# Blocks 0 and 1 of a retention-plus-FFN kernel in units of 256 tokens and four heads, with two tokens per partition

## The chip, the cores and the metric

The kernel runs on one core of a Trainium2 chip. The metric is the device time of one execution in microseconds (us); of several runs the median is taken.

## The reference

Two layers follow each other. The first is a recurrent attention with decay (retention): for 4 batches, 8 heads, 768 tokens and a head dimension of 64, a 64 x 64 state per head is decayed by gamma and takes up the outer product of k and v at each token; y is q times the state. The second is a feed-forward pair over the 3072 tokens, with x of 512 columns (8 heads x 64), 2048 hidden columns, and a PReLU whose slope for negative values is alpha.

```python
for t in range(S):
    state = gamma[None, :, None, None] * state + np.einsum('bhd,bhe->bhde', k[:, :, t], v[:, :, t])
    y[:, :, t] = scale * np.einsum('bhd,bhde->bhe', q[:, :, t], state)
...
h = x @ w_in
g = np.maximum(h, 0.0) + alpha * np.minimum(h, 0.0)
return (g @ w_out).astype(np.float32)
```

Inputs and output are float32; the kernel computes its matmuls in float16 with float32 sums.

## The kernel before, in words

The recurrence is cut into chunks of 128 tokens. Within a chunk it is a masked product of scores; between chunks a state per pair of heads is carried. A unit u is one chunk of one batch with all 8 heads, 24 units in all; four units make a block of 512 tokens, and the feed-forward pair runs once per block (`ffn1`, `ffn2`; six blocks).

For each unit:

- `load` (L109) issues three DMAs of 256 KB on SP's queue: k, q, v, one token per partition, so that each packet is one token of one head, 256 bytes. Eight buffers per tensor.
- `prep` scales k (L127, on VectorE for the first two blocks, later on GpSimd) and q (L135, GpSimd) by the decay tables into `kdq`, and casts v into `vx` (L149, GpSimd). `vx` has a block of zeros in the middle, so that a 128-column slice of it holds one head of a pair and zeros for the other.
- `stage_a` turns k and q (eight 128 x 128 transposes on TensorE, L168, for the first 10 units, a transposing DMA for the others), ScalarE copies the result to `kq` (L175), and k times v gives the chunk's state in PSUM (`stp`, L181). VectorE adds it to the carried state (L193, L197, two calls of 64 rows, the diagonal 64 x 64 squares alone), GpSimd multiplies by the decay of 128 tokens (L199) into `tg`, the state for the next chunk.
- `stage_b` computes the scores (L214, eight matmuls that each use 64 of TensorE's rows) and masks them on VectorE (L224).
- `stage_c` computes y transposed (L239, L246 within the chunk, L254 from the carried state) into `yps`; ScalarE copies it to `xT` (L264).

`ffn1` runs 16 hidden tiles with four 512-column matmuls each (L282); ScalarE (L292) and VectorE (L293) form the PReLU into `gt`. `ffn2` (L321) sums 16 tiles for four groups of 128 tokens, ScalarE evacuates (L330) and issues the store (L334). With parts=4 it goes through the 16 tiles in four rounds, so that a round needs one quarter of w_out.

Each engine takes its instructions in the order in which the program issues them, written out by hand here: `tick(gen, m)` issues the next m matmuls of a generator, with the stages of attention between such pieces. `keep(m)` issues m spin matmuls (L95) on data that nothing uses. In block 0 the units run before any feed-forward work, each with keep(5). The weights come over GpSimd's queue: w_in in five DMAs (L361), w_out in four quarters (L365). Their issues stand between GpSimd's own products. The loads of units 4 to 11 wait on SP until the first quarter of w_out has landed (`held`). While ffn2 of block n runs, the units of block n+1 are computed. PSUM has two groups of four banks, "pa" (attention) and "pb" (ffn); a tile takes the next bank of its group when its last user is done.

Of the kernel before, what the change touches and what calls it, by code (L numbers as in the profile page):

```python
# [9 lines left out]
FP = mybir.dt.float32  # L10
# [8 lines left out]
def kernel(  # L19
# [27 lines left out]
    NTAB = 2 * H + NP + 16  # L47
# [4 lines left out]
    for p in range(NP):  # L52
        tab_np[0:64, 2 * H + p] = g64[2 * p] ** 128
        tab_np[64:128, 2 * H + p] = g64[2 * p + 1] ** 128
    tab_np[0:NFT, NTAB - 16 : NTAB] = np.eye(NFT)
    tab_np = tab_np.astype(np.float32)
    mi_np = np.zeros((128, 256), dtype=np.float16)
    mi_np[:, 0:128] = p_ar[:, None] <= p_ar[None, :]
    mi_np[:, 128:256] = np.eye(128)

# [8 lines left out]
    mi = sbp.tile([128, 256], F16, tag="mi", name="mi")  # L69
    mask = mi[:, 0:128]  # L70
    ident = mi[:, 128:256]
    alpha_sb = sbp.tile([NFT, 128], FP, tag="alpha", name="alpha")
# [8 lines left out]
    NPE = 10  # L81
    vext = [sbp.tile([128, NP, 3, 64], F16, tag=f"vx{i}", name=f"vx{i}") for i in range(NV)]
# [21 lines left out]
    def load(u):  # L104
        b, c = divmod(u, NCH)
        t = {}
        for nm, src in (("k", k), ("q", q), ("v", v)):
            t[nm] = sbp.tile([128, H, D], FP, tag=f"{nm}s", bufs=8, name=f"{nm}s{u}")
            ins = nc.sync.dma_start(  # L109
                out=t[nm],  # L110
                in_=src[b, :, C * c : C * c + C, :].rearrange("h p d -> p h d"),
            )
# [11 lines left out]
    def prep(u, ahead=None, amid=None, behind=None):  # L124
        t = staged.pop(u)
        kdq = sbp.tile([128, 2, H, D], F16, tag="kdq", bufs=8, name=f"kdq{u}")
        (nc.vector if u < 2 * UB else nc.gpsimd).tensor_tensor(  # L127
            out=kdq[:, 0],
            in0=t["k"],
            in1=tab[:, 0:H].unsqueeze(2).to_broadcast([128, H, D]),  # L130
            op=MULT,
        )
        if ahead:
            ahead()
        nc.gpsimd.tensor_tensor(  # L135
            out=kdq[:, 1],
            in0=t["q"],
            in1=tab[:, H : 2 * H].unsqueeze(2).to_broadcast([128, H, D]),
            op=MULT,
        )  # L140
        if amid:
            amid()
# [10 lines left out]
        if behind:  # L153
            behind()
# [6 lines left out]
    def stage_a(u):  # L161
# [16 lines left out]
        if c < NCH - 1:  # L178
# [11 lines left out]
            for lh in range(2):  # L190
                s = slice(64 * lh, 64 * lh + 64)
                if c > 0:
                    nc.vector.tensor_tensor(  # L193
                        out=new[s, :, s], in0=tgs[u][s, :, s], in1=stv[s, :, s], op=ADD
                    )
                else:
                    nc.vector.tensor_copy(out=new[s, :, s], in_=stv[s, :, s])  # L197
# [148 lines left out]
    for u in range(UB):  # L346
        load(u)
# [149 lines left out]
```

## Time and profile before

| what | us |
|---|---|
| three runs: median (lowest, highest) | 230.56 (229.25, 231.67) |
| the profiled execution, its own time | 228.91 |
| its span, first to last instruction | 227.1 |
| TensorE busy | 211.8 |
| VectorE busy | 124.8 |
| ScalarE busy | 96.1 |
| GpSimd busy | 83.1 |
| first transposes of units 0, 1, 2, 3 (L168) | 6.20, 9.82, 13.28, 17.12 |
| first matmul of ffn1, of ffn2 in block 0 (L282, L321) | 21.51, 36.25 |
| first transpose of block 2, right behind ffn1 of block 1 | 77.69 |
| last evacuation (L330) starts | 223.07 |

In the profile, PE is TensorE, PEld its weight loads, DVE VectorE, ACT ScalarE, POOL GpSimd, SP the queue of the loads. A row of the groups names line, engine, operation, tiles and shapes, then total busy time and the mean duration of one in ns, then the idle time ahead of it and what ended it. The slices cut the span into 40 equal parts and give the busy share in tenths. The chain follows the work that ended last back to its start. The DMA view gives packets, megabytes, and the time of the packets as a share of 16 engines over the window; several packets of one engine can be in flight, so the shares can add up to more than 100%.

### The profile page before, as it was taken

To read this page: it belongs to the slowest core of one execution; us is meant where nothing else is said; L and a number is where in the kernel's file an instruction comes from. 1 tells how busy PE (TensorE), PEld (TensorE's weight loads), DVE (VectorE), ACT (ScalarE), POOL (GpSimd) and SP (SyncE) were. 2 spreads that over 40 slices of the span, in tenths; PEclk is the share of its full clock that TensorE was granted. 3 is DMA by queue.
4 is the path that set the end of the run, shared out by engine and by line. 5 is a ranking of instruction groups with operands and counts; after the bars stand their busy time and mean duration, and the time that the engine had idled before them with its cause. 6 is when DMAs were issued, how large, how long until landed. Compare 5 with 4: busy or idle time off the path is not lost.

```text
span 227.1 us, 3793 instructions
## 1 busy us (share of the span) xinstructions
PE 211.8 (93%) x1454; PEld 108.5 (48%) x1454; DVE 124.8 (55%) x203; ACT 96.1 (42%) x156; POOL 83.1 (37%) x99
## 2 busy tenths in 40 slices
PE   7786998949889999999999999999999999999992
PEld 2454644525454555544455544455544555544440
DVE  4485496431539845248855268834288834288100
ACT  2242673411737732256522367323376231566121
POOL 2689302632496134950031990104970230000000
PEclk9999999999999999999999999999999999999999
DMA  7999999998999999699911399931470011100111
GB/s 156 218 200 160 199 189 225 207 186 182 283 275 218 193 211 253 154 263 226 198 48 49 93 245 224 229 92 46 104 161 15 0 62 58 67 3 0 46 66 73
DMA packets 98209, 33.36 MB, mean 147 GB/s; under 512 B 90368, under 2 KB 95120, under 8 KB 98192
## 3 DMA queue, kind: packets, MB, share of 16 engines
q1 hardware_dynamic: 89664, 22.55, 50.6%
q0 software_dynamic: 4752, 4.19, 12.1%
q10 hardware_dynamic: 3776, 6.39, 7.9%
q8 instruction: 11, 0.18, 0.3%
q14 instruction: 6, 0.05, 0.1%
HBM read 27.36 MB, written 6.29 MB: 148 GB/s over the span
## 4 chain that ended last, share of the span: by engine, by line
PE 73%; DMA 13%; POOL 5%; SPq 4%; ACT 2%; issue 1%; ACTq 0%; POOLq 0%
PE ops L321 33%; PE hps L282 31%; DMA wout<-in_moe_w_out_dram 8%; DMA qs<-in_q_dram 4%; SPq L109 4%; PE sca L214 3%; PE yps L246 2%; PE yps L239 2%; PE yps L254 1%; POOL win L361 1%; POOL kdq L135 1%; POOL tg L199 1%; PE stp L181 1%; ACT kq L175 1%; ACT os L330 1%
## 5 line engine op out<-in xcount | busy, mean ns | idle before, releaser
L321 PE MATMUL ops<-wout,gt 128*128 128x512 f16 x384 | 92.5, 379 | 3.1 <-DMA wout<-in_moe_w_out_dram 3.1
L293 DVE SCALAR_TENSOR_TENSOR gt<-hm,oma,hps 128x512 f16<-128x512 f32 x96 | 69.8, 746 | 31.2 <-ACT hm L292 23.3
L282 PE MATMUL hps<-xT,win 128*128 128x512 f16 (+2 forms) x416 | 84.6, 363 | 1.7 <-ACT xT L264 1.7
L292 ACT ACTIVATE hm<-hps 128x512 f32<-128x512 f32 x96 | 56.7, 597 | 23.4 <-PE hps L282 22.8
L282 PEld LDWEIGHTS <-win 128*128 128x128 f16 x416 | 39.3, 98 | 45.3 <-issue 2.5
L321 PEld LDWEIGHTS <-gt 128*128 128x128 f16 x384 | 34.5, 98 | 38.0 <-issue 3.7
L199 POOL TENSOR_TENSOR tg<-ss,tab 128x512 f16<-128x512 f32 x20 | 20.9, 1043 | 70.7 <-DVE ss L193 50.2
L135 POOL TENSOR_TENSOR kdq<-qs,tab 128x512 f16<-128x512 f32 x24 | 25.3, 1054 | 30.3 <-DMA qs<-in_q_dram 30.3
L330 ACT ACTIVATE os<-ops 128x512 f32<-128x512 f32 x24 | 14.3, 596 | 46.3 <-PE ops L321 42.8
L224 DVE TENSOR_TENSOR m<-sca,mi 128x512 f16<-128x512 f32 x24 | 16.6, 691 | 28.4 <-PE scb L214 28.1
L264 ACT ACTIVATE xT<-yps 128x512 f16<-128x512 f32 x24 | 14.3, 597 | 36.2 <-PE yps L254 32.1
L175 ACT ACTIVATE kq<-trb 128x1024 f16<-128x1024 f16 x10 | 10.2, 1024 | 19.4 <-PE trb L168 18.9
L193 DVE TENSOR_TENSOR ss<-tg,stp 64x256 f32<-64x256 f16 x32 | 13.4, 418 | 8.5 <-PE stp L181 5.6
L127 POOL TENSOR_TENSOR kdq<-ks,tab 128x512 f16<-128x512 f32 x16 | 16.7, 1044 | 0.4 <-DMA ks<-in_k_dram 0.4
L239 PE MATMUL yps<-m,vx 128*128 128x128 f16 x96 | 16.8, 219 | 0.0
L246 PE MATMUL yps<-m,vx 128*128 128x128 f16 x96 | 16.6, 219 | 0.0
L224 DVE TENSOR_TENSOR m<-scb,mi 128x512 f16<-128x512 f32 x24 | 16.3, 680 | 0.0
L149 POOL CAST vx<-vs 128x512 f16<-128x512 f32 x24 | 14.7, 612 | 2.0 <-DMA vs<-in_v_dram 1.7
L127 DVE TENSOR_TENSOR kdq<-ks,tab 128x512 f16<-128x512 f32 x8 | 6.4, 800 | 14.7 <-DMA ks<-in_k_dram 14.7
L254 PE MATMUL yps<-kq,tg 128*128 128x128 f16 x80 | 14.4, 219 | 0.0
L246 PEld LDWEIGHTS <-vx 128*128 128x128 f16 x96 | 9.4, 98 | 2.3
L239 PEld LDWEIGHTS <-vx 128*128 128x128 f16 x96 | 9.4, 98 | 2.3
(26 smaller groups left out, 85.2 us busy)
## 6 DMA issues: line engine op xcount, KB each, us to landing
ks<-in_k_dram SPq DMA_DIRECT2D x24, 256.0 KB, 4.4
qs<-in_q_dram SPq DMA_DIRECT2D x24, 256.0 KB, 4.7
vs<-in_v_dram SPq DMA_DIRECT2D x24, 256.0 KB, 5.1
out_dram<-os ACTq DMA_DIRECT2D x24, 256.0 KB, 2.0
wout<-in_moe_w_out_dram POOLq DMA_DIRECT2D x4, 512.0 KB, 10.3
win<-in_moe_w_in_dram POOLq DMA_DIRECT2D x3, 512.0 KB, 6.8
win<-in_moe_w_in_dram POOLq DMA_DIRECT2D x2, 256.0 KB, 4.6
kq<-kdq SPq DMA_TRANSPOSE x14, 4.1
```

The lines of the kernel that those rows point to most:

```text
L127: (nc.vector if u < 2 * UB else nc.gpsimd).tensor_tensor(out=kdq[:, 0], in0=t["k"], in1=tab[:, 0:H].unsqueeze(2).to_broadcast([128, H, D]) ...
L135: nc.gpsimd.tensor_tensor(out=kdq[:, 1], in0=t["q"], in1=tab[:, H : 2 * H].unsqueeze(2).to_broadcast([128, H, D]), op=MULT,)
L199: nc.gpsimd.tensor_tensor(out=tg, in0=new, in1=tab[:, 2 * H : 2 * H + NP].unsqueeze(2).to_broadcast([128, NP, 128]), op=MULT,)
L224: nc.vector.tensor_tensor(out=m2, in0=scs[lh].rearrange("p (a i) -> p a i", i=128), in1=mask.unsqueeze(1).to_broadcast([128, NP, 128]), op ...
L239: nc.tensor.matmul(out=o, lhsT=vx[:, p, 0:2, :].rearrange("p a d -> p (a d)"), rhs=m2s[0][:, p, :], start=True, stop=False,)
L246: nc.tensor.matmul(out=o, lhsT=vx[:, p, 1:3, :].rearrange("p a d -> p (a d)"), rhs=m2s[1][:, p, :], start=False, stop=(c == 0),)
L254: nc.tensor.matmul(out=o, lhsT=tgs[u][:, p, :], rhs=kq[:, 512 + 128 * p : 512 + 128 * p + 128], start=False, stop=True,)
L282: nc.tensor.matmul(out=hpss[ft][:, lo:hi], lhsT=w_in_all[:, hp, 128 * ft : 128 * ft + 128], rhs=xT[n][:, hp, lo:hi], start=(hp == 0), stop ...
L292: nc.scalar.activation(out=hm, in_=hps, func=RELU, bias=0.0, scale=-1.0)
L293: nc.vector.scalar_tensor_tensor(out=gt[:, ft, :], in0=hm, scalar=oma_sb[:, ft : ft + 1], in1=hps, op0=MULT, op1=ADD,)
L321: nc.tensor.matmul(out=opss[tq], lhsT=gt[:, ft, 128 * tq : 128 * tq + 128], rhs=w_out_all[:, ft, :], start=(ft == 0), stop=(ft == NFT - 1),)
L330: nc.scalar.activation(out=os_sb, in_=opss[tq], func=COPY, bias=0.0, scale=1.0)
```

## The change

Blocks 0 and 1 get units of another shape. Unit i = 2j + g is 256 tokens (chunks 2j and 2j+1) of four heads (group g), the same 256 KB per tensor. A partition holds two neighbouring tokens, so a packet is 512 bytes. The first 64 partitions are the first chunk (half 0), the others the second (half 1); s tells the even from the odd token. The attention of such a unit uses 64-row matmuls for the state (`u_state`) and for the part within the chunk (`u_out`), and 64 x 64 tiles for the scores (`u_scores`). `u_turn` does the transposes, in block 0 with ScalarE's copy in two pieces (parts=2). `uprep` scales k on VectorE and q on GpSimd; v is cast on ScalarE in block 0, on GpSimd in block 1.

Beside that: five units are loaded ahead of the weights instead of four; w_in comes in four DMAs of 512 KB, the first after q's product of unit 3, the other three after the state product of unit 3; in all units the state is added in one call over 128 x 512 (or 128 x 256) with the off-diagonal squares, which the product with the new table `gmat` sets to zero; the first part of `ffn1` in blocks 0 and 1 starts with one hidden tile over 256 tokens instead of four over 384; and block 1's pieces stand at other places in ffn2 of block 0. Blocks 2 to 5 keep their units and their order.

The diff, cut to its core ("..." marks what is left out):

```diff
         for nm, src in (("k", k), ("q", q), ("v", v)):
+            st = sbp.tile([128, H * D], FP, tag=f"{nm}s", bufs=8, name=f"{nm}s{u}")
+            if u < NUN:
+                j, g = divmod(u, 2)
+                b, c = divmod(2 * j, NCH)
+                t[nm] = st.rearrange("p (h s d) -> p s h d", s=2, d=D)
+                ins = nc.sync.dma_start(
+                    out=st.rearrange("p (h x) -> p h x", h=H // 2),
+                    in_=src[
+                        b, H // 2 * g : H // 2 * g + H // 2, C * c : C * c + 2 * C, :
+                    ].rearrange("h (p s) d -> p h (s d)", s=2),
+                )
...
                 )
             new = sst[u % NT]
             stv = stp.rearrange("p (a e) -> p a e", e=128)
-            for lh in range(2):
-                s = slice(64 * lh, 64 * lh + 64)
-                if c > 0:
...
+            if c > 0:
+                nc.vector.tensor_tensor(out=new, in0=tgs[u], in1=stv, op=ADD)
+            else:
+                nc.vector.tensor_copy(out=new, in_=stv)
+            tg = sbp.tile([128, NP, 128], F16, tag="tg", bufs=4, name=f"tg{u}")
+            nc.gpsimd.tensor_tensor(out=tg, in0=new, in1=gmat, op=MULT)
             tgs[u + 1] = tg
...
+    def uprep(i, amid=None, behind=None, cast=None):
...
+        for a, (eng, nm) in enumerate(((nc.vector, "k"), (nc.gpsimd, "q"))):
+            o = TU + 2 * H * a
+            eng.tensor_tensor(
+                out=kdu[:, a],
+                in0=t[nm],
+                in1=tab[:, o : o + 2 * H]
+                .rearrange("p (s h) -> p s h", s=2)[:, :, H // 2 * g : H // 2 * g + H // 2]
+                .unsqueeze(3)
+                .to_broadcast([128, 2, H // 2, D]),
+                op=MULT,
+            )
+        if amid:
+            amid()
+        vx = vext[i % NV].rearrange("p (s r) x d -> p s r x d", s=2)
+
...
+    def u_turn(i, tag="pa", parts=1):
+        kdu, kq, vx, cast_v = prepped[i]
+        trb = ps("trb", F16, 1024, tag=tag)
+        for x in range(2 * NP):
+            a, s, r = x // NP, x // 2 % 2, x % 2
+            nc.tensor.transpose(
+                out=trb[:, 128 * x : 128 * x + 128],
+                in_=kdu[:, a, s, 2 * r : 2 * r + 2, :].rearrange("p a d -> p (a d)"),
+                identity=ident,
+            )
+            if (x + 1) % (2 * NP // parts) == 0:
+                lo = 128 * (x + 1 - 2 * NP // parts)
+                hi = 128 * (x + 1)
+                nc.scalar.activation(
+                    out=kq.rearrange("p a i -> p (a i)")[:, lo:hi],
+                    in_=trb[:, lo:hi],
+                    func=COPY,
+                    bias=0.0,
+                    scale=1.0,
+                )
+
+    def u_state(i, tagb="pa"):
+        j, g = divmod(i, 2)
+        kdu, kq, vx, cast_v = prepped[i]
+        ua = 2 * j
+        b, ca = divmod(ua, NCH)
+        halves = (0, 1) if ca + 1 < NCH - 1 else (0,)
+        stps = [ps("stp", tag=("pa", tagb)[hf]) for hf in halves]
+        for r in range(2):
+            for s in range(2):
+                for hf in halves:
+                    z = slice(64 * hf, 64 * hf + 64)
+                    nc.tensor.matmul(
+                        out=stps[hf][:, 128 * r : 128 * r + 128],
+                        lhsT=kdu[z, 0, s, 2 * r : 2 * r + 2, :].rearrange("p a d -> p (a d)"),
+                        rhs=vx[z, s, r, 0::2, :],
+                        start=(s == 0),
+                        stop=(s == 1),
+                    )
+
+        def advance(hf):
+            if hf not in halves:
+                return
...
+            new = sst[hf][:, gs, :]
+            stv = stps[hf][:, 0:256].rearrange("p (a e) -> p a e", e=128)
+            if u % NCH:
+                nc.vector.tensor_tensor(out=new, in0=tgs[u][:, gs, :], in1=stv, op=ADD)
+            else:
+                nc.vector.tensor_copy(out=new, in_=stv)
+            if u + 1 not in tgs:
+                tgs[u + 1] = sbp.tile([128, NP, 128], F16, tag="tg", bufs=4, name=f"tg{u}")
+            nc.gpsimd.tensor_tensor(
+                out=tgs[u + 1][:, gs, :], in0=new, in1=gmat[:, gs, :], op=MULT
+            )
+
+        return advance
+
+    def u_scores(i):
+        kdu, kq, vx, cast_v = prepped[i]
+        kqv = kq.rearrange("p (a s r) i -> p a s r i", a=2, s=2)
+        scs = [ps("sca"), ps("scb")]
+        for r in range(2):
+            for s in range(2):
+                for hf in range(2):
+                    z = slice(64 * hf, 64 * hf + 64)
+                    for lh in range(2):
+                        y = slice(64 * lh, 64 * lh + 64)
+                        c0 = 256 * s + 128 * r
+                        nc.tensor.matmul(
+                            out=scs[lh][z, c0 : c0 + 128],
+                            lhsT=kqv[y, 0, s, r, z],
+                            rhs=kqv[y, 1, :, r, z],
+                            start=True,
+                            stop=True,
+                        )
+        m2s = []
+        live[i] = (kqv, vx, m2s)
+
+        def masked(lh):
+            m2 = sbp.tile([128, NP, 128], F16, tag=f"m2{lh}", bufs=2, name=f"m2{lh}")
+            m2 = m2.rearrange("p (s r) i -> p s r i", s=2)
+            nc.vector.tensor_tensor(
+                out=m2,
+                in0=scs[lh].rearrange("p (s r i) -> p s r i", s=2, r=2),
+                in1=masku.unsqueeze(2).to_broadcast([128, 2, 2, 128]),
+                op=MULT,
+            )
+            m2s.append(m2)
+
...
+    def u_out(i):
...
+        def put(hf, r, lhsT, rhs):
+            seen[hf] += 1
+            nc.tensor.matmul(
+                out=ypss[hf][:, 128 * r : 128 * r + 128],
+                lhsT=lhsT,
+                rhs=rhs,
+                start=(seen[hf] == 1),
+                stop=(seen[hf] == total[hf]),
+                skip_group_check=True,
+            )
+
+        for lh in range(2):
+            for r in range(2):
+                for s in range(2):
+                    for hf in range(2):
+                        z = slice(64 * hf, 64 * hf + 64)
+                        put(
+                            hf,
+                            r,
+                            vx[z, s, r, lh : lh + 2, :].rearrange("p a d -> p (a d)"),
+                            m2s[lh][z, s, r, :],
+                        )
+        for hf in range(2):
+            z = slice(64 * hf, 64 * hf + 64)
+            for r in range(2):
+                if inter[hf]:
+                    put(hf, r, tgs[2 * j + hf][:, 2 * g + r, :], kqv[:, 1, :, r, z])
...
+        for hf in range(2):
+            c0 = C * (2 * jj + hf)
+            nc.scalar.activation(
+                out=xT[n][:, 2 * g : 2 * g + 2, c0 : c0 + C].rearrange(
+                    "p a (i s) -> p a s i", s=2
+                ),
+                in_=ypss[hf][:, 0:256].rearrange("p (a s i) -> p a s i", a=2, s=2),
+                func=COPY,
+                bias=0.0,
+                scale=1.0,
+            )
...
         for ft in range(early):
             hpss[ft] = ps("hps", tag="pb")
-            yield from product(ft, 0, TB - C)
+            yield from product(ft, 0, TB // 2)
+            yield from product(ft, TB // 2, TB, range(2))
         for ft in range(early):
-            yield from product(ft, TB - C, TB)
+            yield from product(ft, TB // 2, TB, range(2, 4))
...
-    for u in range(UB):
+    for u in range(UB + 1):
         load(u)
...
+    uprep(0)
+    uprep(1)
     keep(14)
+    ends = {}
+    for i in range(UB):
+        u_turn(i, tag="pb", parts=2)
+        prepped[i][3](nc.scalar)
+        if i < UB - 1:
+            m = u_scores(i)
+            m(0)
+            m(1)
+            if i:
+                u_out(i - 1)
+            if i == 0:
...
             keep(5)
+            ends[i] = u_state(i, tagb="pb" if i > 1 else "pa")
+            ends[i](0)
+            if i + 2 < UB:
+                uprep(i + 2)
+            if i + 2 == UB - 1:
+                get_wi(0, 4)
+            if i < UB - 2:
+                ends.pop(i)(1)
+        else:
+            m = u_scores(i)
+            ends[i] = u_state(i, tagb="pb")
+            m(0)
+            ends[i](0)
+            m(1)
+            u_out(i - 1)
+    get_wi(4, 8)
+    get_wi(8, 12)
+    get_wi(12, 16)
     held.append(get_wo(0))
+    ends.pop(2)(1)
+    ends.pop(3)(1)
     get_wo(1)
-    for u in range(UB, 3 * UB):
+    for u in range(UB + 1, 3 * UB):
         load(u)
 
-    gen = ffn1(0, early=4)
-    tick(gen, 8)
-    stage_c(UB - 1)
+    gen = ffn1(0, early=1)
+    tick(gen, 6)
+    u_out(UB - 1)
     for _ in gen:
         pass
     gen = ffn2(0, parts=4)
-    prep(4)
-    prep(5, amid=lambda: get_wo(2), behind=lambda: get_wo(3))
+    def u_begin(i):
+        u_turn(i)
+        ends[i] = u_state(i)
+        ends[i](0)
+
+    def u_mid(i):
+        m = u_scores(i)
+        m(0)
+        m(1)
+        ends.pop(i)(1)
+    uprep(4, cast=nc.gpsimd)
+    uprep(5, amid=lambda: get_wo(2), cast=nc.gpsimd)
     tick(gen, 9)
-    stage_a(4)
-    tick(gen, 5)
-    stage_b(4)
+    u_begin(4)
+    tick(gen, 6)
+    u_mid(4)
+    uprep(6, cast=nc.gpsimd)
+    tick(gen, 8)
+    u_begin(5)
+    tick(gen, 2)
+    u_out(4)
     tick(gen, 4)
-    stage_a(5)
+    u_mid(5)
+    uprep(7, amid=lambda: get_wo(3), cast=nc.gpsimd)
+    tick(gen, 8)
+    u_begin(6)
+    tick(gen, 2)
+    u_out(5)
     tick(gen, 4)
-    stage_c(4)
-    tick(gen, 3)
+    u_mid(6)
+    tick(gen, 8)
+    u_begin(7)
+    tick(gen, 2)
+    u_out(6)
     tick(gen, 4)
-    stage_a(7)
-    stage_c(6)
+    u_mid(7)
     for _ in gen:
         pass
-    gen = ffn1(1, early=4)
-    tick(gen, 8)
-    stage_b(7)
-    tick(gen, 8)
-    stage_c(7)
+    gen = ffn1(1, early=1)
+    tick(gen, 6)
+    u_out(7)
```

## Prediction

> **What bounds the kernel now.** I read the page from the top: busy times, slices, then the chain of work that ended last, then timeline, windows and DMA view of the first 78 us, the only part that the change touches.
>
> ```profile
> span 227.1 us, 3793 instructions
> ...
> PE 211.8 (93%) x1454; PEld 108.5 (48%) x1454; DVE 124.8 (55%) x203; ACT 96.1 (42%) x156; POOL 83.1 (37%) x99
> ...
> PE   7786998949889999999999999999999999999992
> ...
> DMA  7999999998999999699911399931470011100111
> ```
>
> PE is full from slice 14 on (from 77 us; a slice is 5.7 us), at a granted clock of 0.999. Only the first 13 slices have holes, and there the DMA row is full. The chain says which transfers end those holes:
>
> ```profile
> 7.67 5.12 DMA qs<-in_q_dram
> ...
> 23.20 9.84 DMA wout<-in_moe_w_out_dram
> ...
> 36.55 5.00 DMA qs<-in_q_dram
> ...
> 42.61 8.53 DMA wout<-in_moe_w_out_dram
> 51.17 4.59 PE ops L321 x20
> ...
> 66.18 11.51 PE hps L282 x64
> 77.69 0.45 PE trb L168 x8
> ```
>
> Left column: start; middle: length. The loads of q, the first w_out quarter (they hold back block 1's loads), and the third w_out quarter set the pace. By the timeline ffn1(0) ends and ffn2(0) starts at 36.25, and PE then stands 3.15 us until 51.17. At 77.69 ffn1(1) is done; from there PE never waits again. So I work out two marks of the changed kernel: the end of ffn1(0) (now 36.25) and of ffn1(1) (now 77.69). The rest must shift by what the second mark shifts.
>
> Durations that I use:
>
> ```profile
> L292 ACT ACTIVATE hm<-hps 128x512 f32<-128x512 f32 x96 | 56.7, 597 | 23.4 <-PE hps L282 22.8
> L199 POOL TENSOR_TENSOR tg<-ss,tab 128x512 f16<-128x512 f32 x20 | 20.9, 1043 | 70.7 <-DVE ss L193 50.2
> L224 DVE TENSOR_TENSOR m<-sca,mi 128x512 f16<-128x512 f32 x24 | 16.6, 691 | 28.4 <-PE scb L214 28.1
> L175 ACT ACTIVATE kq<-trb 128x1024 f16<-128x1024 f16 x10 | 10.2, 1024 | 19.4 <-PE trb L168 18.9
> L193 DVE TENSOR_TENSOR ss<-tg,stp 64x256 f32<-64x256 f16 x32 | 13.4, 418 | 8.5 <-PE stp L181 5.6
> ```
>
> ACT takes 0.597 us for 512 columns and 1.024 for 1024, so 0.17 + 0.83 per 1000: 256 columns 0.385. A 512-column matmul holds PE 0.216 us (64 in 13.81), a 128-column one 0.055 (4 stp in 0.22), a pair of 64-row ones 0.055 together, since L214's sca and scb start in the same instant.
>
> **Part by part.**
>
> *Loads, 512-byte packets.* In 3 to 4 us two queues run side by side, q1 with 256-byte load packets, q10 with the 512-byte rows of the mask:
>
> ```profile
> q1 hardware_dynamic: 831, 0.21, 93.4%
> q10 hardware_dynamic: 145, 0.07, 23.5%
> ```
>
> Share x 16 engines x 1 us / packets: 18.0 ns against 25.9 ns. One load is 64 packets per engine now (64 x 18.0 = 1.15; the windows of 8 to 16 us move 218 GB/s, 1.20 us per 256 KB), then 32 (32 x 25.9 = 0.83; with the same 4% over, 0.86). Bounds 0.60 (a packet costs the same at any size) and 1.20 (bytes cost all); I take 0.86, from the row that has the size itself. Fifteen loads, with unit 4's, then are through by about 15 (1.9 + 0.25 for the mask + 15 x 0.86); now twelve take until 16.5. The Trainium skill's page "DMA: Bandwidth & Descriptors", section Specifications, asks 512 B for line rate and gives about 27 GiB/s per engine: by it, as an estimate, a load would take 0.57 us, and the sum would come out at rival 1's 231.0 instead of 233.1.
>
> *Block 0's loop, the term that speaks against the change.* The first unit can't start before the spin matmuls end: k's transposes start at 6.20 now, and will. From then on the order written on PE is one chain per unit. In the built program the second four transposes of u_turn wait for ACT's copy of the first four (same PSUM tile), so the two halves don't overlap: 0.40 (four transposes with their drain) + 0.60 + 0.40 + 0.60 + four hand-overs of about 0.05 = 2.18. Scores: 16 matmuls at 0.028 = 0.45, and 0.11 to enter and leave the small tiles (eight sca/scb stand 0.33 apart from their neighbours, 79.87 to 80.20, for 0.22 of work) = 0.56. u_out of the unit before: 16 x 0.028 + 4 x 0.055 + 0.11 = 0.78. keep(5): five spin matmuls, 1.08. u_state: 8 x 0.028 + 0.11 = 0.33. Sum 4.93 per unit. Now units follow at 3.5 to 3.8 us, and what ends those waits is the next load; afterwards loads come every 2.6 us and wait for PE. The spin matmuls, which now fill a wait, lie on the path.
>
> Transposes of units 0 to 3 thus start at 6.2, 10.4, 15.3, 20.3. Now they start at 6.2, 9.8, 13.3, 17.1. Unit 3: kq at 22.45, masks done 23.8 and 24.5; out2 waits for the first mask (its PSUM bank), to 24.6; xT two copies of 0.385, to 25.5; two ticks; out3, 26.5; xT3, 27.4. From there 0.22 + 15 x 0.864 = 13.2 of ffn1(0): 40.6.
>
> *POOL's queue and the weights.* Three of four w_in issues move behind the state product of unit 3, which waits for DVE: m3a 23.8, ss 0.42, product about 0.55 (half of 1043 ns), so the first issues at 24.85, where now the last goes out by 22.2. From issue start to landing: 1.6 to the first packet, 2.7 for 512 KB at 190 GB/s (windows 22 to 34 us), 1.4 until a waiter sees it: 30.5. PE wants it at 30.2: a stall of 0.3, ffn1(0) ends at 40.9, that is 4.65 later than now. Queued behind these issues are the products (2,1), (3,1), wanted at 48, and the first w_out, which lands at 24.85 + 1.6 + 4 x 2.7 + 1.4 = 38.7 (now 33.1): SP's held loads of units 5 to 7 start then, 5.6 later.
>
> *Block 1.* Without waits: ffn2(0) 64 x 0.216 = 13.8, ffn1(1) 13.8, four units of 0.78 (turn and state) + 0.56 + 0.78 = 8.5, k4's product on DVE after the last gt 0.2, xT7 0.9: 37.2. Now the same stretch takes 41.45; unit 4 is there early, and no wait for k4 and q4 remains. Gain 4.25.
> POOL issues w_out 2 after q5's product, w_out 3 after q7's. q5 lands at about 43 (now q4's product starts 5.0 after SP is let go; two loads, each 0.34 shorter, make it 4.3), product to 44, issue 44, landing 8.5 later by the chain's 8.53 (bounds 6.6, w_in's median, and 11.7, w_out's longest): 52.5. PE wants it after 32 ticks, at 51.4: stall 1.1. q7 needs five more loads beside that transfer and lands at about 49.5; product 1.04, issue 50.6, landing 59.1; PE, pushed by 1.1, wants it at 58.1: stall 1.0. Together 2.1 (bounds 0 and 5).
>
> *Everything else.* Blocks 2 to 5: DVE's two 64-row additions (836 ns) become one over 128 x 512, costed at m's 691; PE covers both, and where PE weren't full it would be 0.15 per unit. POOL's product reads a full table instead of a broadcast: 1043 both. Two more copies and one memset on POOL before 4 us lie under the wait for q0. The bigger mask is 64 KB, 0.25 us of DMA, under the spin matmuls. xT's strided write and v's cast on ACT: 0.6 in slots where PE works. Zero together (bounds -0.5 and +0.5).
>
> Sum: +4.65 - 4.25 + 2.1 = +2.5 at the second mark. The profiled execution took 228.91 (span 227.1 and 1.8 around it), so 231.4; the median of the runs shown, 230.56, is 1.65 higher, so 233.1, 1.1% slower. A measurement can tell about 1%, 2.3 us.
>
> Entering and leaving the small tiles costs 0.11 by L214's rows and is in the sum three times per unit; paid once, it would take 0.22 from each of eight units. The rule behind that row, and against this change, is the Trainium skill's: its page "TensorEngine Tiling (Array Packing)", section Key Properties, says that a change of tiling mode drains TensorE. Without that rule the sum would be 231.3, by it and the row it is 233.1. Its section Restrictions adds that column tiling switches fast weight load off, which no row here shows.
>
> **Rivals.**
> 1. *Weights in time, not slower.* If q7 lands three us sooner, both w_out stalls go: 233.1 - 2.1 = 231.0. For it: loads at the lower bound of 0.60 bring seven loads (k5 to q7) 1.8 us sooner, and w_out 3 alone on the queues may need 6.6 instead of 8.5. Against it: k7, issued at 42.40, came only at 54.5 beside w_out. It decides if w_out 3 lands before 57.0.
> 2. *Small tiles don't run side by side.* Halves of rows do (sca and scb), halves of columns are shown nowhere. At 0.055 instead of 0.028 the 16 score matmuls cost 0.45 more per unit, eight units 3.6: 236.7.
> 3. *The packets don't help.* At 1.20 per load nothing in block 0 changes (PE's chain is longer), but q7 comes seven times 0.34 = 2.4 later, and w_out 3 with it: 235.5.
> 4. *Block 0 follows the loads.* If the loop ran at 3.6 us like now, ffn1(0) would end 1.33 x 3 = 4.0 sooner: 229.1, and with rival 1's stalls gone 227.0. Against it stands the sum of 4.93 from rows that scatter little.
>
> **How the numbers follow.** Forecast 0.45, spread 231 to 235 by the stalls' bounds: 0.27 of it slower by over 1%, 0.18 within. Rival 1: 0.22, of it 0.20 within and 0.02 faster. Rival 2: 0.14, slower. Rival 3: 0.08, slower. Rival 4: 0.11, of it 0.09 faster and 0.02 within. Faster 0.11, same 0.40, slower 0.49. Range: from 229.0, at rival 4, to 237.0, just above rival 2; left out are double gains and a state matmul that doesn't pair either.
>
> **What the profile would show.** Right: load packets near 26 ns; trb of units 1 to 3 about 4.9 us apart, with kps ended by nothing but PE's own order; DMA holes between 15 and 26 us; ops starting near 41; two short waits of PE for wout; 128-row work of blocks 2 to 5 unchanged at 32.7 us per block. Wrong: trb spaced under 4 us (rival 4), sca of one unit over 0.8 us long (rival 2), no PE wait for wout (rival 1).

## The result and the profile after

The changed kernel takes 239.08 us (median of four executions, 238.52 to 239.23) where the kernel before takes 229.91: a ratio of 1.038, with a 95% interval of 1.031 to 1.045. The profiled execution took 239.23 us, its span is 237.5. The forecast was 233.1 with a range of 229.0 to 237.0. It had the sign, and it missed the size by 6 us. Executions of one kernel differ in their mean granted clock (0.971 to 0.986 here); so the kernels below are compared by profiles too, at the two marks of the prediction, and their clock stands beside them. Ratios here and below are to the kernel before, timed beside each kernel, and leave out executions that took over 1.5% longer than the fastest of their kernel; medians hold all.

The page's first lines answer to those shown of before (a slice is 5.9 us here):

```profile
span 237.5 us, 4041 instructions
...
PE 215.7 (91%) x1586; PEld 108.2 (46%) x1586; DVE 123.5 (52%) x190; ACT 100.9 (42%) x172; POOL 87.1 (37%) x102
...
PE   7667799989626999999999999999999999999993
...
PEclk9999999999985999999999999999999999999999
DMA  6955899999999870269971159981192011100112
```

Slices 11 to 13, that is 59 to 77 us, are new: TensorE at 0.6, 0.2 and 0.6, and its clock falls in slices 12 and 13. The DMA row has got holes early (slices 3 and 4), where before it was full. The chain of waits names what ended the hole:

```profile
13.61 1.08 PE kps L111 x5
15.02 0.34 PE trb L321 x4
...
26.28 11.23 DMA wout<-in_moe_w_out_dram
...
43.78 8.02 DMA wout<-in_moe_w_out_dram
51.84 1.24 PE ops L510 x5
...
61.74 10.16 DMA qs<-in_q_dram x2
...
71.98 0.38 ACTq L523
...
73.22 14.88 PE hps L470 x62
88.11 0.45 PE trb L185 x8
```

Up to 58 us it is the picture of the prediction: spin matmuls on the path, then w_out. Then come two loads of q, and behind them not a product that reads q, but ACTq L523: the issue of an output store. The first mark (the first block's second product begins) is at 40.15, 3.90 later than before; the second (the transposes of block 2 begin) at 88.11, 10.42 later. From there to the end both kernels need 149.4 us.

ACT's timeline around the hole (start, length, engine, line; in brackets the idle time ahead and what ended it):

```profile
58.90 1.02 ACT L329 ACTIVATE kq<-trb 128x1024 f16<-128x1024 f16 x1 [2.84 <-PE trb L321]
59.82 0.59 ACT L519 ACTIVATE os<-ops 128x512 f32<-128x512 f32 x1
62.66 0.40 ACTq L523 DMA_DIRECT2D out_dram<-os  x1
63.11 0.76 ACT L450 ACTIVATE xT<-yps 128x256 f16<-128x256 f32 x2 [2.70 <-DMA qs<-in_q_dram]
63.72 0.60 ACT L519 ACTIVATE os<-ops 128x512 f32<-128x512 f32 x1
65.53 0.36 ACTq L523 DMA_DIRECT2D out_dram<-os  x1
65.94 0.60 ACT L519 ACTIVATE os<-ops 128x512 f32<-128x512 f32 x1 [1.62 <-PE ops L510]
68.01 0.35 ACTq L523 DMA_DIRECT2D out_dram<-os  x1
68.40 0.60 ACT L519 ACTIVATE os<-ops 128x512 f32<-128x512 f32 x1 [1.87 <-DMA vs<-in_v_dram]
71.98 0.38 ACTq L523 DMA_DIRECT2D out_dram<-os  x1
72.41 0.76 ACT L450 ACTIVATE xT<-yps 128x256 f16<-128x256 f32 x2 [3.41 <-DMA qs<-in_q_dram]
```

Read it by the gap ahead of each ACTq. The tile os is full at 60.4, its store goes out at 62.66; the last one is full at 69.0 and goes out at 71.98. In between ACT stands, and all that is queued behind stands with it: the copies of xT6 and xT7 (xT of units 6 and 7), which don't read any q. TensorE waits for them, for xT6 since it holds the PSUM bank of the next scores, for xT7 since `ffn1` reads it (the numbers are us in total, times, longest):

```profile
PE hps L470 <- ACT xT L450: 6.1, 1, 6.1
ACT xT L450 <- DMA qs<-in_q_dram: 6.1, 2, 3.4
...
PE scb L386 <- ACT xT L450: 2.1, 1, 2.1
```

The built program says what a store has to do with a load. The loads on SP's queue and the stores on ACT's share eight completion semaphores (counters that a transfer raises when it has landed), dealt out in turn; a transfer is issued only when the one that had its semaphore before has landed. In the kernel before, the four stores of ffn2(0) follow k7, v7, q8 and q9. In the changed kernel they follow q10, k11, v11 and q12: in the order in which the semaphores are dealt out 39 loads stand ahead of the first store, where 29 did. SP's queue gets to q10's load at 57.89 only and to q12's at 65.48, and it takes 4.8 and 6.5 us from there until a store is let go. The loads themselves are not later than before: there, q10's goes out at 62.43. New is which load a store waits for.

### The profile page after: what moved, and what is told of

Read it like the earlier page. It is cut to its first block, busy times and chain, and to the rows that moved or that the text cites. A ratio compares the mean times of both kernels' runs of the same rounds, so it can differ in the third digit from the quotient of the medians.

```text
span 237.5 us, 4041 instructions
## 1 busy us (share of the span) xinstructions
PE 215.7 (91%) x1586; PEld 108.2 (46%) x1586; DVE 123.5 (52%) x190; ACT 100.9 (42%) x172; POOL 87.1 (37%) x102
## 4 chain that ended last, share of the span: by engine, by line
PE 77%; DMA 14%; ACT 3%; POOL 2%; issue 1%; SPq 1%; DVE 1%; ACTq 0%
PE ops L510 32%; PE hps L470 30%; DMA wout<-in_moe_w_out_dram 8%; DMA qs<-in_q_dram 6%; PE kps L111 3%; ACT kq L329 2%; PE sca L222 2%; PE trb L321 2%; PE yps L247 2%; PE yps L254 2%; PE yps L262 1%; PE stp L198 1%; PE yps L420 1%; POOL win L555 1%; PE sca L386 1%
## 5 line engine op out<-in xcount | busy, mean ns | idle before, releaser
L481 DVE SCALAR_TENSOR_TENSOR gt<-hm,oma,hps 128x512 f16<-128x512 f32 x96 | 71.4, 747 | 41.3 <-ACT hm L480 31.6
L470 PE MATMUL hps<-xT,win 128*128 128x512 f16 (+1 forms) x392 | 85.9, 379 | 7.5 <-ACT xT L450 7.5
L470 PEld LDWEIGHTS <-win 128*128 128x128 f16 x392 | 38.7, 99 | 53.3 <-issue 9.8
L212 POOL TENSOR_TENSOR tg<-ss,gmat 128x512 f16<-128x512 f32 x13 | 16.5, 1268 | 73.4 <-DVE ss L208 53.7
L272 ACT ACTIVATE xT<-yps 128x512 f16<-128x512 f32 x16 | 9.6, 597 | 25.7 <-PE yps L262 21.8
L369 POOL TENSOR_TENSOR tg<-ss,gmat 128x256 f16<-128x256 f32 x14 | 10.9, 787 | 19.5 <-DVE ss L366 7.3
L329 ACT ACTIVATE kq<-trb 128x512 f16<-128x512 f16 (+1 forms) x12 | 8.9, 740 | 21.1 <-PE trb L321 21.1
L247 PE MATMUL yps<-m,vx 128*128 128x128 f16 x64 | 11.2, 219 | 0.0
L254 PE MATMUL yps<-m,vx 128*128 128x128 f16 x64 | 11.2, 219 | 0.0
L450 ACT ACTIVATE xT<-yps 128x256 f16<-128x256 f32 x16 | 6.1, 451 | 11.7 <-DMA qs<-in_q_dram 6.1
L232 DVE TENSOR_TENSOR m<-scb,mi 128x512 f16<-128x512 f32 x16 | 10.9, 681 | 0.0
L208 DVE TENSOR_TENSOR ss<-tg,stp 128x512 f32<-128x512 f16 x11 | 7.5, 686 | 5.4 <-PE stp L198 5.4
L262 PE MATMUL yps<-kq,tg 128*128 128x128 f16 x56 | 10.1, 219 | 0.0
```

The source lines that it names most:

```text
L212: nc.gpsimd.tensor_tensor(out=tg, in0=new, in1=gmat, op=MULT)
L232: nc.vector.tensor_tensor(out=m2, in0=scs[lh].rearrange("p (a i) -> p a i", i=128), in1=mask.unsqueeze(1).to_broadcast([128, NP, 128]), op ...
L247: nc.tensor.matmul(out=o, lhsT=vx[:, p, 0:2, :].rearrange("p a d -> p (a d)"), rhs=m2s[0][:, p, :], start=True, stop=False,)
L254: nc.tensor.matmul(out=o, lhsT=vx[:, p, 1:3, :].rearrange("p a d -> p (a d)"), rhs=m2s[1][:, p, :], start=False, stop=(c == 0),)
L262: nc.tensor.matmul(out=o, lhsT=tgs[u][:, p, :], rhs=kq[:, 512 + 128 * p : 512 + 128 * p + 128], start=False, stop=True,)
L329: nc.scalar.activation(out=kq.rearrange("p a i -> p (a i)")[:, lo:hi], in_=trb[:, lo:hi], func=COPY, bias=0.0, scale=1.0,)
```

## Experiments

Theory T1: ACT's queue, blocked by stores whose semaphores belong to late loads, makes xT6 and xT7 late, and the hole costs once more through the clock. T2: block 0's longer loop, or late data, is the cost. T3: the small tiles are. L lines and names are those of the changed kernel; where a run adds lines, the same code stands a few lines further down.

### The stores off ACT's queue

```
-                        nc.scalar.dma_start(out=out[row : row + 128, :], in_=os_sb)
+                        (nc.scalar if n else nc.gpsimd).dma_start(out=out[row : row + 128, :], in_=os_sb)
```

> Only change against the changed kernel: the four output stores of the first block's second product go out on POOL's queue, not on ACT's, so that ACT no longer stands in front of a store that waits for the semaphore lane of a late load. Theory T1 (ACT's queue, blocked by those waits, makes xT6 and xT7 late): xT7 is copied at about 67, as soon as its matmuls end, the transposes of block 2 start near 80 to 81 where they now start at 88.1, and the time is 239.1 - 7.5 = 231.6. Rival T2 (the loads of units 8 to 13 are themselves late and PE waits for data, or block 0's longer loop is the whole cost): no move, 239. Rival T3 (small tiles or their mode changes cost the time): no move, 239.

The same with `nc.sync` in place of `nc.gpsimd`:

> The same four stores on SP's queue, behind the loads of unit 11, so that SP and not ACT waits for the lanes. T1: the same as with POOL's queue, 231.6, since six buffers hold the stored tiles and nothing needs them early; up to 1 us more if the loads of units 12 to 15, now behind the stores, come too late for block 3. T2 and T3: 239.

On POOL's queue: 232.0 us, ratio 1.010 [0.995, 1.025]; 229.17 and 231.36 in the two executions with a mean clock of 0.999 and more. On SP's queue: 230.16 in the execution with clock 1.00, which was profiled, and 233.8 to 234.9 at 0.975 to 0.978. ACT's timeline with the stores on SP's queue:

```profile
60.06 0.59 ACT L519 ACTIVATE os<-ops 128x512 f32<-128x512 f32 x1
60.56 0.77 ACT L450 ACTIVATE xT<-yps 128x256 f16<-128x256 f32 x2
61.45 0.60 ACT L519 ACTIVATE os<-ops 128x512 f32<-128x512 f32 x1
...
64.83 0.76 ACT L450 ACTIVATE xT<-yps 128x256 f16<-128x256 f32 x2 [0.61 <-PE yps L420]
66.06 0.60 ACT L480 ACTIVATE hm<-hps 128x512 f32<-128x512 f32 x1 [0.47 <-PE hps L470]
```

xT6 is copied right behind os, xT7 when its matmuls end. Marks: 39.91 and 78.97, 9.1 earlier at the second. T1 holds; T2 and T3 can't explain these 9.1 us. What is left against before is 1.28 at the second mark (the prediction had 2.5).

### The hole filled with spin matmuls

```
     u_out(7)
+    keep(24)
```

> The changed kernel with 24 spin matmuls (5.2 us at full clock) put on TensorE behind the last output product of block 1, where it stands still for 6.1 us; the stores stay on ACT. If the gap costs twice, once as a wait and once by the lower clock after it (0.68 in the ten us from 70), the wait stays and the clock does not fall: the first product of block 1 needs 13.4 instead of 14.9 and the time is 237.6. If the lower clock is only a reading and costs nothing: 239.1. If the spin matmuls end after xT7 is there: up to 240.

238.22 us, ratio 1.045 [1.034, 1.056]; 237.15 in the profiled execution, at clock 1.00. In the changed kernel the clock falls in the hole and stays low behind it, first by the windows of that kernel (the column before the last two is the clock), then by the chain of the one with spins:

```profile
64.00:68.00 4.00, 3.08 (x33) 1.77 (x32) 1.62 (x3) 0.92 (x2) 2.24 (x3) 1.00 1.07 273
68.00:72.00 4.00, 0.00 (x0) 0.00 (x0) 0.00 (x0) 0.60 (x1) 4.00 (x6) 0.70 0.96 265
72.00:76.00 4.00, 2.78 (x8) 1.16 (x8) 0.75 (x1) 1.81 (x4) 4.00 (x5) 0.50 0.93 241
```

```profile
72.70 13.33 PE hps L470 x62
```

The same 62 matmuls take 13.33 where they took 14.88: the fall costs 1.55. As a median that gain does not show: the ratio is no better than that of the changed kernel. But the clock fell in two of the four executions all the same: they took 239.28 and 239.81 at 0.991 and 0.986, the other two 236.84 and 237.15 at 0.998 and 1.00. The wait stays, as expected (the spins end at 71.9, and xT7 is copied from 71.9 to 72.7); against the stores on SP's queue, on the same chip, both at clock 1.00, the second mark is at 86.03 and not 78.97. So ACT's wait alone is worth 7.06 us.

### Without the spin matmuls of block 0's loop

Stores on POOL's queue, and:

```
-            keep(5)
```

> The stores on POOL's queue as in the first run, and the five spin matmuls per unit of block 0's loop left out (three times 1.08 us). The prediction's sum has them on the path: the first block's second product would start at 36.9 where it now starts at 40.15, and what of these 3.2 us the weights let through comes off the end: 228.4 to 231.6 where the first run stands at 231.6. If they only fill waits for ACT, DVE or POOL: no move. If TensorE's clock falls without them: slower, up to 3 us.

233.23 us, ratio 1.025 [1.015, 1.035], with the clock at 0.946 to 0.954 in all four executions. The prediction put these spins on the path, and they are; but they hold the clock. The columns are window, then busy time and count of PE, PEld, DVE, ACT and POOL, then clock:

```profile
10.00:15.00 5.00, 3.62 (x50) 2.41 (x50) 3.51 (x9) 2.37 (x6) 3.16 (x4) 0.66 1.06 318
15.00:20.00 5.00, 3.60 (x50) 2.54 (x50) 2.28 (x5) 2.53 (x6) 3.67 (x5) 0.50 0.33 42
```

The clock is at 0.50 from 12 to 32 us, and the first mark comes at 43.47. The same fall, shorter, hit the kernel with the stores on POOL's queue; there the longest wait of TensorE from 18 to 24 us was only 0.7 us:

```profile
20.00:22.00 2.00, 1.31 (x18) 0.77 (x17) 0.42 (x1) 0.60 (x1) 0.95 (x2) 1.00 0.88 109
22.00:24.00 2.00, 0.97 (x30) 0.77 (x31) 0.84 (x2) 1.12 (x2) 0.00 (x0) 0.92 0.93 153
24.00:28.00 4.00, 3.58 (x41) 2.52 (x40) 1.44 (x4) 0.76 (x2) 3.74 (x6) 0.50 0.30 42
28.00:32.00 4.00, 3.37 (x18) 1.51 (x15) 0.75 (x1) 1.57 (x4) 3.74 (x5) 0.50 1.24 205
```

The stretch ahead of the fall is one of thin work, unit 3's transposes and copies without spins: 2.28 of 4 us busy from 20 to 24. That alone does not decide it: in the changed kernel's profile the same 4 us hold 2.28 too, and the clock stayed at 1.00. The Trainium skill's page "TensorE: Matmul & The Clock Gate", section "Why this matters for your kernels", warns of idle gaps over about 3 us; these rows show a fall with no wait over 0.7 us, and here the measurement decides.

### Spin matmuls in the waits

Stores on SP's queue, no spins behind the scores, and in u_turn two behind each half's copy:

```
-            keep(5)
...
+                if parts == 2:
+                    keep(2)
```

> Stores on SP's queue; in block 0's loop, in its old order, the five spin matmuls behind the scores are gone and two stand behind each half of the transposes, in the 0.6 us in which TensorE waits for ACT's copy. Theory that the granted clock falls to 0.50 for some 10 us when two us in a row hold under 0.4 us of matmuls each (as at 21 to 23 us in the run with the stores on POOL's queue, and from 7 us on without spin matmuls): the spins in the waits keep the clock at 1.0 in all executions, and the chain of a unit is 1.1 us shorter, 3.6 instead of 4.7: units 3.6 apart, the first block's second product starts at 36.5 to 37.5 (40.15 in the changed kernel), end 227 to 229. Theory that the clock falls by the work of the whole stretch and not by its gaps: it falls still, 231 to 235.

228.48 us, ratio 1.000 [0.996, 1.004], and the clock at 0.996 or more in all ten executions, where the old loop with the stores off ACT had it at 0.975 to 0.978 in four of eight. First mark 38.72 (36.5 to 37.5 expected; the first unit began 1.0 later, and the second unit's transposes are 4.4 from the third's, not 3.6), second 78.24. Without spins the clock fell in four of four, with spins between the work in four of eight, with spins in the waits in none of ten. That points to the gaps and not to the work of the whole stretch; but the ten ran on another chip than the others, and that this makes no difference is not shown. And the change, rid of ACT's wait and of the falls, makes no difference to the kernel before that can be measured.

### Weights earlier, and packets, in the old loop

Stores on SP's queue, and:

```
             if i + 2 == UB - 1:
                 get_wi(0, 4)
+                get_wi(4, 8)
+                get_wi(8, 12)
+                get_wi(12, 16)
...
-    get_wi(4, 8)
-    get_wi(8, 12)
-    get_wi(12, 16)
```

> Stores on SP's queue and the four quarters of w_in issued early, with block 0's loop in the old order. If only the late weights cost block 1 its time: w_out's first quarter lands about 5 us sooner (32), the waits for the third quarter go, and the end moves by 1 to 2 us, to 228 to 229 at full clock. If block 0's loop holds everything back by itself: no move, 230.2.

Stores on SP's queue, and for units 0 to 7:

```
-                    out=st.rearrange("p (h x) -> p h x", h=H // 2),
-                    in_=src[
-                        b, H // 2 * g : H // 2 * g + H // 2, C * c : C * c + 2 * C, :
-                    ].rearrange("h (p s) d -> p h (s d)", s=2),
+                    out=st.rearrange("p (h d) -> p h d", d=D),
+                    in_=src[b, :, C * c : C * c + C, :].rearrange("h p d -> p h d"),
```

> Stores on SP's queue, and the loads of units 0 to 7 with 256-byte packets again: 64 packets per engine for 256 KB where there were 32. The kernel reads one token of each of eight heads per partition into the same tiles, so it computes on other data than it should; all instructions stay. If the packets are what they seem to be (0.8 us per 256 KB against 1.20): block 0 does not move, since its chain on TensorE is longer than the loads, and in block 1 the product of q5 comes 2 us later and the third quarter of w_out with it; end 231 to 233 at full clock where 512-byte packets give 230.2. If the packets buy nothing that ends on the path: 230.2.

235.36 us, ratio 1.033 [1.025, 1.041], and 235.7 us, ratio 1.032 [1.026, 1.038]. In both the clock was at 0.971 to 0.985 in every execution, and in the profiles at 0.50 from 25 to 30 us and under 1.0 for some us on either side; first marks 45.02 and 44.20. Neither says what it was made for: beside such a fall a microsecond can't be read. The packets were tried again below.

### Block 0's loop in another order

Stores on SP's queue; a second PSUM tile for the second half of u_turn, and another order in the loop (in the last unit likewise):

```
+            if parts == 2 and x == NP:
+                trb = ps("trb", F16, 1024, tag=tag)
...
+            if i:
+                u_out(i - 1)
             m = u_scores(i)
             m(0)
             m(1)
-            if i:
-                u_out(i - 1)
```

> On top of the stores on SP's queue: in block 0's loop the output product of the unit before moves between the transposes and the scores of the unit (where TensorE waits for ACT's copies), and the two halves of the transposes get a PSUM tile each, so that the copy of the first runs beside the transposes of the second. The spin matmuls stay. By the prediction's term for the loop (2.18 us of serialized transposes and copies, 0.78 of output product behind them, each unit 4.7 apart in the profiles) a unit takes about 3.1: transposes 0.65, output product 0.8, scores 0.2, spin matmuls 1.1, state 0.33. The transposes of unit 3 start near 15.5 (now 19.5), the first block's second product 4 us sooner unless w_in is late, and the end moves from 230.2 at full clock to 226 to 230. If the loads or DVE and POOL set the 4.7 instead: no move.

The same with w_in's four quarters issued together, by the diff shown for that above:

> The run before it with the four quarters of w_in issued together behind unit 3's product of q in POOL's queue, instead of three of them behind the last state products. Theory that the weights, issued late, are what block 0's loop costs: the DMA hole between 15 and 20 us (12 GB/s in the changed kernel) closes, the first quarter of w_out lands at 31 to 33 instead of 37.2, the loads of units 5 to 7 start with it, and the time is 224 to 227. Theory that TensorE's chain alone sets the pace: as the run before, within 1 us.

230.43 us, ratio 1.011 [1.005, 1.017]; first mark 41.01, with the clock at 0.50 from 25 to 30 us; the first units are 3.6 and 4.1 apart, where 3.1 was expected. With w_in: 230.3 us, ratio 1.003 [0.999, 1.008]; marks 39.28 and 78.28 at a mean clock of 0.996, but five of the ten executions at 0.981 to 0.984. The first lies just above its range, the second within 1 us of the first; but the clock differs between them, so what the early weights are worth is not shown. In the second, the output product issued in unit 3 stands 1.8 us for a state product that POOL makes behind four issues of w_in (17.66 to 20.82): the DMA hole closed in part (75 and 197 GB/s from 15 to 20 and from 20 to 25 us, where there were 12 and 103), and the wait moved into POOL's queue.

### The loop written anew

Stores on SP's queue, two PSUM tiles in u_turn, and this order behind the transposes of each unit, the last one included (the other issues of w_in in the loop and behind it go, but for the last quarter's):

```
+        ends[i] = u_state(i, tagb="pb")
+        ends[i](0)
+        if i:
+            u_out(i - 1)
+        m = u_scores(i)
+        m(0)
+        m(1)
...
+        keep(3)
+        if i + 1 < UB:
+            prepped[i + 1][3](nc.scalar)
+        if i + 2 < UB:
+            uprep(i + 2)
+        if i > 0:
+            get_wi(4 * i - 4, 4 * i)
+        ends.pop(i)(1)
```

> Stores on SP's queue and a block-0 loop written anew: a PSUM tile for each half of the transposes, then the unit's state product and the output product of the unit before (both in the wait for ACT's copies), then scores and three spin matmuls; ACT casts v one unit ahead; one quarter of w_in issued per unit from the second on. If block 0's loop is what the change still costs (end of the first block's first product at 40.15 against 36.25), a unit takes about 3.0 to 3.3 us, bound by ACT, DVE and POOL alike (each some 2.9 us of work per unit), that product ends at 34 to 36, and the time is 224 to 227, below the kernel before. If the weights set the pace (8.4 MB of loads and weights have to come in by 45 us), the gain stops at 227.

225.52 us, ratio 0.985 [0.979, 0.992], clock 0.998 or more in all four. The units are 3.4 to 3.6 apart:

```profile
7.21 0.61 PE L323 MATMUL trb<-mi,kdq 128*128 128x128 f16 x8
...
10.79 0.61 PE L323 MATMUL trb<-mi,kdq 128*128 128x128 f16 x8
...
14.21 0.61 PE L323 MATMUL trb<-mi,kdq 128*128 128x128 f16 x8
...
17.58 0.61 PE L323 MATMUL trb<-mi,kdq 128*128 128x128 f16 x8
```

Marks 36.42 and 76.48, against 36.25 and 77.69 before. The time is in the range expected, the spacing and the first mark a little above theirs. A version that beats both, if by little.

### The stores back on ACT, and 256-byte packets, in the new loop

The new loop with the stores on ACT's queue:

```
-                        (nc.scalar if n else nc.sync).dma_start(out=out[row : row + 128, :], in_=os_sb)
+                        nc.scalar.dma_start(out=out[row : row + 128, :], in_=os_sb)
```

> The rewritten loop with the four stores of the first block back on ACT's queue; nothing else differs from that run. If ACT standing in front of the lanes of late loads is the main cost of the change, it must cost again although block 0 is short: PE waits 5 to 8 us for xT6 and xT7 between 60 and 72 and the ratio to the kernel before goes from 0.985 to 1.01 or 1.02. If the first run's gain came from the stores' transfers (elsewhere in time, other contention) and not from ACT's wait: within 1% of 0.985.

232.65 us, ratio 1.015 [1.009, 1.022]: 3.0% worse for where four stores are issued.

```profile
60.49 0.34 ACTq L525 DMA_DIRECT2D out_dram<-os  x1
60.88 0.60 ACT L521 ACTIVATE os<-ops 128x512 f32<-128x512 f32 x1 [2.30 <-DMA qs<-in_q_dram]
62.87 0.34 ACTq L525 DMA_DIRECT2D out_dram<-os  x1
63.25 0.60 ACT L521 ACTIVATE os<-ops 128x512 f32<-128x512 f32 x1 [1.77 <-DMA ks<-in_k_dram]
64.69 0.34 ACTq L525 DMA_DIRECT2D out_dram<-os  x1
65.08 0.76 ACT L452 ACTIVATE xT<-yps 128x256 f16<-128x256 f32 x2 [1.24 <-DMA qs<-in_q_dram]
```

The first marks agree (35.99 and 36.42); the second is 81.30, not 76.48. The matmuls of ffn1(1) take 15.41 there and 13.33 with the stores on SP's queue: 2.1 of the 5 us are the clock again; TensorE waits 4.5 us for xT7 and 0.8 for xT6. T1 holds with the short block 0 too.

The new loop, stores on SP's queue, with the diff shown above for 256-byte packets:

> The rewritten loop with stores on SP's queue, and loads of units 0 to 7 in 256-byte packets (one token of each of eight heads per partition: the kernel computes on other data than it should; instructions as before). If the packets' price is real and the new loop is as fast as the loads: at 1.0 to 1.2 us per 256 KB the product of q3 comes 12 x 0.2 to 0.4 = 2.4 to 4.8 us later, the end 2 to 4 us later, ratio 0.995 to 1.005. If engines and not loads set the new loop: below 0.5%, that is no change against 0.985.

232.12 us, ratio 1.018 [1.010, 1.025]; marks 41.96 and 79.92. The units' transposes follow at 3.1 to 3.6 us all the same. What comes late is w_in, issued on POOL behind the product of q3, and the clock falls in the wait for it (0.50 from 25 to 30 us), which the expectation had not counted:

```profile
23.54 0.83 PE L478 MATMUL hps<-xT,win 128*128 128x256 f16 x6 [2.93 <-DMA win<-in_moe_w_in_dram]
```

There the packets are worth 3.4 us at the second mark, wait and clock together.

### The weights earlier in the new loop, and the kernel before with its stores moved

```
     get_wo(1)
+    get_wo(2)
...
-    uprep(5, amid=lambda: get_wo(2), cast=nc.gpsimd)
+    uprep(5, amid=lambda: get_wo(3), cast=nc.gpsimd)
...
-    uprep(7, amid=lambda: get_wo(3), cast=nc.gpsimd)
+    uprep(7, cast=nc.gpsimd)
```

> The rewritten loop with stores on SP's queue, and the third and fourth quarter of w_out issued one stage earlier in POOL's queue: the third behind the second, the fourth behind the product of q5 where the third stood. In the run before TensorE waits 1.8 us for the fourth quarter (52.5 to 55.4 holds work for 1.1 us). If only the issue is late: that wait goes and the end moves by 1.8 us, ratio 0.977. If the queues are full there (200 to 320 GB/s) and the loads of units 5 to 7 come later instead by the 2.7 us of a quarter: no gain or a loss of up to 2 us, 0.985 to 0.994.

225.01 us, ratio 0.984 [0.979, 0.989]: no gain over 0.985.

The kernel before with its first block's stores on SP's queue:

```
-                        nc.scalar.dma_start(out=out[row : row + 128, :], in_=os_sb)
+                        (nc.scalar if n else nc.sync).dma_start(out=out[row : row + 128, :], in_=os_sb)
```

> The kernel before with one change: its first block's four stores on SP's queue. Its profile shows ACT once 3.5 us in front of such a store. If that wait delays xT7 there too (ACT copies it at 65.53, PE is done with it near 65.4): at most 0.3 us faster, that is no change; the mechanism then belongs to the change. If the blocked store also holds back the kernel before: 1 to 3 us faster.

227.06 us, ratio 0.993 [0.988, 0.997]: 1.7 us, neither of the two cases cleanly. Its second mark is 75.00, but 2.1 of these 2.7 us are won before any store goes out: the third quarter of w_out starts TensorE's work at 49.04 there, at 51.17 before. Why is left open. It also bounds the win above: the new loop (0.985 [0.979, 0.992]) and the kernel before with moved stores (0.993 [0.988, 0.997]) have intervals that overlap, so it is not shown that units of 256 tokens beat those of 128.

## Why the prediction was wrong

- **Block 0's loop: right.** Starts of the transposes of units 1 to 3 were forecast at 10.4, 15.3 and 20.3; they are at 10.34, 15.02 and 19.70. A unit takes 4.7 instead of 4.93; the scores were the term that was too dear (0.35 from the first to the next instruction, where 0.56 stood; the 16 starts take 0.21 of it).
- **Loads: right.** From 5 to 14 us 330 GB/s come in (20.6 for each of the 16 engines), 0.79 us per 256 KB, where 218 did; the forecast was 0.86. The 27 GiB/s per engine of the Trainium skill's page "DMA: Bandwidth & Descriptors", section Specifications, from which the prediction worked out 0.57 us, are not reached here.
- **Weights and first mark: right, a little dear.** w_out's first quarter landed at 37.5 (38.7 forecast), the mark is 40.15 (40.9). The stall of 0.3 for w_in did not come.
- **Block 1 without w_out's stalls: nearly right.** 37.2 forecast, with xT7's copy in it; with the stores on SP's queue it is 39.06 with 1.26 of waiting for w_out, so 37.8.
- **Stalls for w_out: half right.** 0.8 for the third quarter in the changed kernel and 1.26 with the stores on SP's queue (1.1 forecast), none for the fourth (1.0).
- **Rivals.** 2, small tiles one after another: wrong, four ran side by side. 3, packets that don't help: wrong for the loads themselves. 4, block 0 following the loads: wrong, TensorE's chain set the pace. 1, weights in time, came nearest to what was left without ACT's wait.
- **"Everything else. ... Zero together": the step that failed.** It costed what ACT gets to do in slots where TensorE works, and not what stands in ACT's queue. The output stores were in no term of the sum, though the change alters which load's semaphore each store must wait for (loads of units 10 to 12 instead of 7 to 9). Which part of the change moves them there, no run isolates. The runs put 7.06 us on that wait and 1.55 on the clock behind it.
- **The clock, taken as 1.0 throughout, failed too.** The forecast's sum had the gaps of each unit in it, and no price for what they do to the clock.

Summed over the two marks: +3.90 for block 0, -2.38 for block 1 without ACT's wait (39.06 against 41.44), +7.06 and +1.55 make 10.13 of the 10.42 measured. Without the last two the second mark would be late by 1.5, close to the 2.5 forecast, in part by luck: block 0 came 0.75 cheaper than forecast and w_out's stalls 0.84, and block 1 gained 0.6 less. The rest, 0.3, is not accounted for; the terms come from different executions.

## What to carry to other kernels

An instruction that issues a transfer is a wait like any other: look up in the built program which earlier transfer's semaphore it takes over, on every queue, whenever a change alters the order of loads and stores. Issue stores from a queue on which nothing urgent stands behind them. And put spin matmuls into TensorE's waits, not between its work: there the clock held in ten executions of ten, and from the first transposes to the first mark block 0 took 31.6 us, where it took 34.0 with the spins between the work.

## What the hardware showed unexpectedly

- Sixteen 64x64 matmuls of 128 columns start within 0.21 us (8.24 to 8.45), one per 14 ns; halves of rows and of columns run side by side, four at a time.
- The granted clock fell to 0.50 with no wait of TensorE over 0.7 us, behind some 3 us of thin work, and then stayed there for about 10 us, through stretches of full work. Another execution with as much work in the same stretch kept its clock.
- The first fourteen spin matmuls take 4.5 to 6.1 us in different executions of these kernels, 0.32 to 0.44 each where a warm one takes 0.216, while the clock's record reads 1.00. The first unit's start moves with them by over 1 us.
- POOL's product of 128x512 takes 1268 ns on average against a full table and 1043 against a broadcast one; costed as equal in the prediction, hidden here, since TensorE's work covers it.
